# Another order of the last step and the tail, earlier accumulating masks and later casts in a top-k attention kernel with a squared-ReLU layer pair

## The chip, the cores and the metric

The kernel runs on one core of one Trainium2 chip. The metric is the device time of one execution in microseconds (us); lower is better. A core has a matrix engine (PE, with PEld for its weight loads), VectorE (DVE), ScalarE (ACT), GpSimd (POOL) and SyncE (SP), which work in parallel. Each takes its own instructions in order and waits for the others through semaphores. Transfers (DMA) are issued by SP, ACT or POOL and run beside the engines.

## The reference, cut to what matters

```python
# q, k, v: (8, 8, 576, 64), float32: batch, heads, rows, head size
scores = scale * np.matmul(q, k.transpose(0, 1, 3, 2))
kth = np.partition(scores, -32, axis=-1)[..., -32:-31]
scores = np.where(scores >= kth, scores, -1000000000.0)     # 32 largest of each row stay
attn = np.exp(scores - np.max(scores, axis=-1, keepdims=True))
attn = attn / (np.sum(attn, axis=-1, keepdims=True) + 1e-09)
x = heads_side_by_side(np.matmul(attn, v))                  # (4608, 512)
h = np.maximum(x @ w_in, 0.0)                               # w_in (512, 2048)
return h * h @ w_out                                        # w_out (2048, 512)
```

## The kernel before, in words

**Steps.** Two heads of a batch make a pair, 32 pairs in all; a pair has nine units of 64 or 128 rows. A step u takes two units at once (x = 0 and 1), and there are U = 144 steps, numbered 0 to 143. Every instruction is written down in a fixed order by the loop over u, and the order within an engine is the order of this program text. The work of one step's units is spread over five turns of the loop:

- in turn u − 1, `scores(u)`: PE multiplies q by k into two PSUM tiles (sc_a, sc_b), ACT copies them into s (L294); DVE's `pairs_of(u)` (L314, L315, and L317 while u is under `EARLY`, which is 11) and POOL's `both(u)` and `lesser(u)` (L338, L347) sort the scores into larger and smaller ones; from step 11 ACT's `copy_far(u)` (L330) moves a quarter of them.
- in turn u, `quads_of(u)` (L323, L324, the first instructions of a step on DVE) and `topk(u)`: four rounds of MAX8 (L373) and three of MATCH_REPLACE8 (L377) on DVE find the 32nd largest.
- in turn u + 1, `drop(u, x)`: ACT negates the maximum and the threshold (neg, L392), POOL writes bytes that mark the scores under the threshold (gone, L407), and these are added to s, which sends those scores far below zero. The addition is one of two: POOL adds by itself for each x (L409), as it does while u is under `EARLY`, or POOL issues one accumulating transfer for both x (L411).
- in turn u + 2, `exps(u, x)` on ACT (L415) and `turn(u)`, a transposing transfer issued by SP (L424).
- in turn u + 4, `products(u)`: PE multiplies by v (L459), `invert(u)` on DVE (reciprocal, L473) and `place(u)` on ACT (L489, L494), which writes the rows of x.

The last two steps are finished without transfers: ACT takes early exponentials (L400), DVE masks them (L419), PE transposes (`turn_by_tensor`, L441), and ACT or DVE copies the result (`turned`, L446, L448).

**q, k and v of a pair** are loaded by SP ahead of time. `prep_units` then gives four units, of which a turn of the loop takes one (two while u is under 8): q transposed, k transposed (`main`, L175), the rest rows (L213 to L216), and `values`, ACT's cast of v (L225). The casts of v's last 64 rows, `last_values` (L221), are put into the list `after_far` by `main` and are done at the end of the same turn.

**The layer pair.** When a chunk of 128 rows of x is complete, `x_unit` lets PE transpose it (L527, copied by ACT at L533 or DVE at L531), and `block` puts four first-layer pieces into `ups` (16 matmuls each, L574, then ReLU on ACT at L579 and the square, L585 on ACT or L583 on DVE). With the last of them four second-layer quarter pieces are put into `downs` (four matmuls each, L617, into the one PSUM tile dn_ps); after the fourth the result is copied (L625 on ACT, in the tail L623 on DVE) and stored by SP. `piece()` takes one entry, from `ups` and `downs` in turn; if the one is empty it takes from the other. With `piece(True)` the part after the matmuls is not done at once but is put into the list `behind`. During the steps `dense` calls `piece` in the gaps of the attention work.

**The tail** is the text after the loop: the products, reciprocals and placements of the last four steps (140 to 143), the last chunk's transposes, all pieces left, a reduction of flags on DVE (L855, which tells whether a slower general path must run), and the last chunk's second layer in two halves of 32 matmuls (L598), copied by DVE (L604) and ACT (L602).

Of the kernel before, what the change touches and what calls it, by code (L numbers as in the profile page):

```python
# [23 lines left out]
def kernel(  # L24
# [66 lines left out]
    raw, prep = {}, {}  # L91

    fetches = []
    after_far = []

    def by_head(t):
        return t.rearrange("p (a d) -> p a d", a=2)
# [61 lines left out]
    def prep_units(i):  # L159
        q_raw, k_raw, v_raw = raw[i]  # L160
        qkT = heads.tile([128, 512 + 640], f32, name="qkT")
        qT, kT = qkT[:, 0:512], qkT[:, 512:1152]
        k_rest = kT.rearrange("p (n d) -> p n d", d=64)[:, 0:10:9]
        bd, va = qbd[i % 5], vau[i % 6]
        prep[i] = (qT, kT, bd, va)

        def twice(t):
            return t.rearrange("p (o d) -> p o d", o=1).broadcast_to([128, 2, 64])

        def main(which, src):  # L170
            def go():
                tp = ps_one.tile([128, 512], f32, name="gen", bufs=2)
                for c in range(4):
                    pin(nc.tensor.transpose(tp[:, c * 128:(c + 1) * 128], src[:, c], id_f[:, :]))
                pin(nc.scalar.activation((qT, kT[:, 64:576])[which], tp[:, :], AF.Copy, scale=(scale, 1.0)[which]))  # L175
                after_far.append(lambda: last_values(which))
            return go


        def first_step():  # L180
            for j, bank in ((0, "gen"), (1, "gen"), (2, "dn_ps"), (3, "sc_a")):
                if bank == "sc_a":
                    tp = ps_sc.tile([128, 2, 512], f32, name=bank)[:, 0, :]
                else:
                    tp = ps_one.tile([128, 512], f32, name=bank, bufs=2 if bank == "gen" else None)
                if j < 2:
                    for c in range(2):
                        pin(nc.tensor.transpose(tp[:, c * 128:(c + 1) * 128], k_raw[:, 2 * j + c], id_f[:, :]))
                    to, got = kT[:, 64 + j * 256:64 + (j + 1) * 256], tp[:, 0:256]
                elif j == 2:  # L190
                    pin(nc.tensor.transpose(tp[:, 0:128], q_raw[:, 0], id_f[:, :]))
                    to, got = qT[:, 0:128], tp[:, 0:128]
                else:
                    pin(nc.tensor.transpose(tp[:, 0:64], k_raw[0:64, 4], id_f[0:64, 0:64]))
                    to, got = k_rest, twice(tp[:, 0:64])
                if j % 2:
                    pin(nc.vector.tensor_copy(to, got))
                else:
                    pin(nc.scalar.activation(to, got, AF.Copy, scale=scale if j == 2 else 1.0))

        def first_q():
            tp = ps_one.tile([128, 512], f32, name="gen", bufs=2)
            for c in range(1, 4):
                pin(nc.tensor.transpose(tp[:, c * 128:(c + 1) * 128], q_raw[:, c], id_f[:, :]))
            pin(nc.scalar.activation(qT[:, 128:512], tp[:, 128:512], AF.Copy, scale=scale))

        def rest(both=(0, 1)):
            tp = ps_one.tile([128, 512], f32, name="gen", bufs=2)
            for which in both:
                src = (q_raw, k_raw)[which]  # L210
                pin(nc.tensor.transpose(tp[:, which * 64:(which + 1) * 64], src[0:64, 4], id_f[0:64, 0:64]))
            if 0 in both:
                pin(nc.scalar.activation(bd[0:64, 0:64], tp[0:64, 0:64], AF.Copy, scale=scale))  # L213
                pin(nc.scalar.activation(bd[64:128, 64:128], tp[64:128, 0:64], AF.Copy, scale=scale))
            if 1 in both:
                pin(nc.scalar.activation(k_rest, twice(tp[:, 64:128]), AF.Copy))  # L216

        def last_values(x):
            assert i < 6 or av_left[i - 6] == 0
            half = slice(64 * x, 64 * x + 64)  # L220
            pin(nc.scalar.activation(va[half, 4 + x, :, 0:64], by_head(v_raw[half, 512:640]), AF.Copy))  # L221

        def values():
            assert i < 6 or av_left[i - 6] == 0
            pin(nc.scalar.activation(va[:, 0:4, :, 0:64], v_raw[:, 0:512].rearrange("p (a c d) -> p c a d", a=2, c=4), AF.Copy))  # L225

        def all_values():
            values()
            last_values(0)
            last_values(1)  # L230

        if i == 0:
            return [first_step, first_q, all_values, lambda: rest((0,))]
        return [main(0, q_raw), main(1, k_raw), rest, values]
# [115 lines left out]
    EARLY = 11  # L350
# [35 lines left out]
    def by_vector(u, x):  # L386
        return u == U - 1 or (u == U - 2 and x == 1)
# [14 lines left out]
    def drop(u, x):  # L402
        d = st[u]
        if x == 0:
            d["neg"] = negate(u, 2)
        s, byte = d["s"], gone[u % 2]
        pin(nc.gpsimd.tensor_scalar(byte[:, x, :, 1], s[:, x, :], scalar1=d["neg"][:, x, 1:2], scalar2=-HUGE, op0=ALU.add, op1=ALU.mult))  # L407
        if by_vector(u, 1) or u < EARLY:
            pin(nc.gpsimd.tensor_tensor(s[:, x, :], s[:, x, :], byte[:, x, :, :].rearrange("p n two -> p (n two)").bitcast(bf16), op=ALU.add))  # L409
        elif x == 1:  # L410
            pin(nc.gpsimd.dma_start(out=s[:, :, :].rearrange("p x n -> p (x n)"), in_=byte[:, :, :, :].rearrange("p x n two -> p (x n two)").bitcast(bf16), accum_op=ALU.add))  # L411
# [59 lines left out]
    def invert(u):  # L471
        r = small.tile([128, 2, 1], f32, name="rsum", bufs=4)
        pin(nc.vector.reciprocal(r[:, :, :], sums(u)[:, :, 64:65]))  # L473
        st[u]["r"] = r
# [265 lines left out]
    def ok(w):  # L740
        return 0 <= w < U
# [6 lines left out]
    def products(w):  # L748
        if ok(w):
            for x in range(2):  # L750
                weigh(w, x)
# [6 lines left out]
    for u in range(U):  # L758
        at_step[0] = u
        for x in range(2):  # L760
            if ok(u - 1) and not by_vector(u - 1, x):
                drop(u - 1, x)
        quads_of(u)
        topk(u, (0,))
        if u == U - 1:
            products(u - 4)
        if ok(u + 1):
            for i, c, a in steps[u + 1]:
                while coming <= i or (coming == i + 1 and soon):
                    prepare(u)  # L770
            scores(u + 1, (lambda: in_gap(u)) if u else None)
            both(u + 1)
        if u == 0:
            in_gap(u)
        if ok(u - 4):
            invert(u - 4)
        casts_next = bool(soon) and soon[0].__name__ == "values"
        for _ in range(0 if casts_next else 2 if u < 8 else 1):
            prepare(u)
        if ok(u - 4):  # L780
            place(u - 4)
        turn_x(u)
        moves.extend(soon_moves)
        soon_moves.clear()
        if u == U - 1:
            moves.pop(0)()()
        if ok(u - 2):
            exps(u - 2, 0)
            exps(u - 2, 1)
            turn(u - 2)  # L790
        fetch(4 if u < 12 else 3)
        topk(u, (1, 2))
        if ok(u + 1):
            pairs_of(u + 1)
            copy_far(u + 1)
            lesser(u + 1)
        topk(u, (3,))
        if casts_next:
            prepare(u)
        while after_far:  # L800
            after_far.pop(0)()
        if u == U - 2:
            early_exps(u, 1)
        if u < U - 1:
            dense(u, 0)
            dense(u, 1)
        else:
            early_exps(u, 0)
            exps(u - 1, 0)
            early_exps(u, 1)  # L810
            piece(True)
            piece(True)
        load_weights(1)
# [3 lines left out]
    while_scores.close()  # L817
    ends["pool"] = fast.enter_context(tc.tile_pool(name="ps_end", bufs=1, space=PSUM))

    def flush():  # L820
        if behind:
            behind.pop(0)()

    assert not fresh and not moves and not soon_moves
    late.append(True)
    products(U - 4)
    piece(True)
    behind.sort(key=lambda go: go.down)
    invert(U - 4)
    for u in (U - 2, U - 1):  # L830
        for x in range(2):
            turn_by_tensor(u, x)
            turned(u, x, u == U - 2)
    products(U - 2)
    products(U - 1)
    place(U - 4)
    products(U - 3)
    invert(U - 2)
    flush()
    place(U - 2)  # L840
    invert(U - 1)
    invert(U - 3)
    flush()
    place(U - 1)
    place(U - 3)
    rest = ups.pop(0)()
    turn_x(U)
    moves.pop(0)()()
    rest()
    while behind:  # L850
        flush()
    tail.append(0)
    while ups:
        ups.pop(0)()()
# [141 lines left out]
```

## Time and profile before

| what | value |
|---|---|
| median of three runs | 917.33 us |
| lowest and highest run | 914.49 and 920.94 us |
| the profiled execution's own time | 915.97 us |
| its span, from the first to the last instruction | 914.1 us |
| DVE busy | 882.7 us, 97% |
| ACT busy | 760.2 us, 83% |
| POOL busy | 777.6 us, 85% |
| PE busy | 675.0 us, 74% |

Rows of the timeline give the start in us, the duration in us, the engine (SPq and the like are an engine's queue of transfers), the line, the operation, output and input by the program's names with shapes, and a count where several instructions were merged; in brackets stands the idle time of the engine just before and what ended it. Rows of the table of stages give the stretch, its length, then busy time and number of instructions of PE, PEld, DVE, ACT and POOL, PE's granted clock (1.00 is full), the share of time that the DMA engines were busy, and GB/s.

### The profile page before, as it was taken

How to read it: one execution, taken by the hardware profiler on the slowest of the kernel's cores; microseconds unless marked ns; L12 is line 12 of the kernel's file. 1: busy time of each engine (PE TensorE's matmuls, PEld its weight loads, DVE VectorE, ACT ScalarE, POOL GpSimd, SP SyncE). 2: the span in 40 equal slices, each digit the busy share in tenths (PEclk: the TensorE clock that was granted, in tenths of full speed). 3: DMA queues.
4: the chain of work that ended last, by engine and by line, in shares of the span. 5: the costliest groups of instructions: out<-in, count | busy, mean ns of one | idle time of the engine just before them, and what ended most of it. 6: DMA issues, size and time to landing. Idle time of an engine off the chain costs nothing.

```text
span 914.1 us, 20885 instructions
## 1 busy us (share of the span) xinstructions
PE 675.0 (74%) x6188; PEld 427.2 (47%) x6264; DVE 882.7 (97%) x3632; ACT 760.2 (83%) x1755; POOL 777.6 (85%) x804
## 2 busy tenths in 40 slices
PE   6667667776786777777786777777777778878776
PEld 3333344544454445444454444454444445545454
DVE  5999999999999999999999999999999999999993
ACT  4566699889888998888987899988998888998881
POOL 7998989888988889888888888998898888888860
PEclk9999999899989999999989999999999999999999
DMA  7698799899998999899899998989989999788851
GB/s 145 106 165 142 155 184 202 192 198 194 193 202 185 196 198 195 190 175 215 178 198 182 202 199 186 205 193 196 185 192 197 199 202 196 156 166 172 163 117 39
DMA packets 290489, 163.60 MB, mean 179 GB/s; under 512 B 258112, under 2 KB 268608, under 8 KB 290368
## 3 DMA queue, kind: packets, MB, share of 16 engines
q1 hardware_dynamic: 267408, 80.29, 47.1%
q0 software_dynamic: 21616, 81.47, 40.0%
q8 instruction: 52, 0.85, 0.4%
q14 instruction: 69, 0.57, 0.2%
q10 hardware_dynamic: 1344, 0.43, 0.2%
HBM read 37.75 MB, written 9.44 MB: 52 GB/s over the span
## 4 chain that ended last, share of the span: by engine, by line
DVE 66%; issue 11%; PE 4%; DMA 3%; ACT 2%; POOL 2%; POOLq 0%; ACTq 0%
DVE m L373 27%; DVE cat L377 18%; DVE sc_b L314 6%; DVE cat L324 5%; DVE cat L323 5%; DVE most L315 4%; DMA s<-gone_a 1%; DMA s<-gone_b 1%; PE dn_ps L617 1%; DVE rsum L473 1%; PE gen L574 1%; PE sc_b L285 1%; POOL gone_b L407 0%; POOL cat L347 0%; PE end L598 0%
## 5 line engine op out<-in xcount | busy, mean ns | idle before, releaser
L373 DVE MAX8 m<-cat 128x8 f32<-128x104 f32 (+3 forms) x1152 | 438.7, 422 | 0.2 <-POOL cat L347 0.2
L377 DVE MATCH_REPLACE8 cat<-m,cat 128x104 f32<-128x104 f32 (+2 forms) x864 | 263.1, 312 | 0.0
L338 POOL TENSOR_TENSOR cat<-s 128x576 int32<-128x576 int32 (+1 forms) x144 | 238.6, 1657 | 3.1 <-ACT s L294 3.1
L347 POOL TENSOR_TENSOR cat<-cat,most 128x576 int32<-128x576 int32 (+1 forms) x144 | 195.8, 1360 | 19.6 <-ACT most L330 7.0
L285 PE MATMUL sc_b<-qkT 64*128 64x288 f32 x512 | 109.1, 501 | 95.3 <-DVE cat L324 91.2
L285 PE MATMUL sc_a<-qkT 64*128 64x288 f32 x512 | 98.2, 456 | 96.6 <-DVE most L315 62.9
L574 PEld LDWEIGHTS <-w_in 128*128 128x128 bf16 x2304 | 146.2, 101 | 39.0 <-issue 17.1
L617 PE MATMUL dn_ps<-w_out,h 128*128 128x512 bf16 x494 | 147.2, 420 | 10.3 <-issue 5.7
L294 ACT ACTIVATE s<-sc_b 128x576 f32<-128x576 f32 x144 | 93.4, 649 | 63.9 <-PE sc_b L285 57.0
L574 PE MATMUL gen<-xT,w_in 128*128 128x128 bf16 x2000 | 138.5, 226 | 2.6 <-ACT xT L533 1.4
L407 POOL TENSOR_SCALAR gone_a<-s,neg 128x576 uint8<-128x576 f32 x143 | 106.6, 745 | 21.3 <-ACT neg L392 10.8
L407 POOL TENSOR_SCALAR gone_b<-s,neg 128x576 uint8<-128x576 f32 x142 | 105.9, 746 | 18.3 <-ACT neg L392 7.7
L285 PEld LDWEIGHTS sc_a<-qkT 64*128 64x128 f32 x512 | 41.8, 188 | 124.2 <-issue 30.7
L285 PEld LDWEIGHTS sc_b<-qkT 64*128 64x128 f32 x512 | 44.7, 201 | 110.7 <-PE av_ps L459 64.1
L294 ACT ACTIVATE s<-sc_a 128x576 f32<-128x576 f32 x144 | 91.0, 632 | 3.3 <-DVE cat L317 1.7
L585 ACT ACTIVATE h<-rl 128x512 bf16<-128x512 f32 x136 | 85.7, 630 | 4.3
L579 ACT ACTIVATE rl<-gen 128x512 f32<-128x512 f32 x141 | 84.0, 596 | 2.4 <-PE gen L574 1.9
L617 PEld LDWEIGHTS <-h 128*128 128x128 bf16 x560 | 54.3, 106 | 66.2 <-issue 32.5
L459 PEld LDWEIGHTS <-wT 128*128 128x128 bf16 (+1 forms) x1600 | 54.9, 100 | 53.6 <-issue 43.9
L411 POOL DMA_DIRECT2D s<-gone_b x66 | 58.4, 884 | 21.7 <-DVE m L373 7.6
L415 ACT ACTIVATE w_two_a<-s,neg 128x576 bf16<-128x576 f32 x96 | 69.4, 781 | 6.7 <-DMA s<-gone_b 4.5
L415 ACT ACTIVATE w_two_c<-s,neg 128x576 bf16<-128x576 f32 x94 | 68.0, 781 | 8.1 <-DMA s<-gone_b 4.7
(170 smaller groups left out, 1203.1 us busy)
## 6 DMA issues: line engine op xcount, KB each, us to landing
s<-gone_b POOLq DMA_DIRECT2D x66, 576.0 KB, 4.6
s<-gone_a POOLq DMA_DIRECT2D x65, 576.0 KB, 4.7
v_raw<-in_v_dram SPq DMA_DIRECT2D x64, 128.0 KB, 3.1
k_raw<-in_k_dram SPq DMA_DIRECT2D x63, 128.0 KB, 3.3
q_raw<-in_q_dram SPq DMA_DIRECT2D x63, 128.0 KB, 3.2
out_dram<-wide SPq DMA_DIRECT2D x31, 256.0 KB, 3.1
v_raw<-in_v_dram SPq DMA_DIRECT2D x64, 32.0 KB, 3.1
w_in<-in_moe_w_in_dram POOLq DMA_DIRECT2D x8, 256.0 KB, 4.8
```

Source lines behind the costliest of these rows:

```text
L285: pin(nc.tensor.matmul(out=ps[j][:, x, 0:HALF], lhsT=lhsT, rhs=rhs, start=True, stop=True))
L294: pin(nc.scalar.activation(s[:, :, j * HALF:(j + 1) * HALF], ps[j][:, :, 0:HALF], AF.Copy))
L338: pin(tt(less, s[:, :, 0:wide].bitcast(i32), s[:, :, HALF:HALF + wide].bitcast(i32), op=ALU.add))
L347: pin(tt(less, less, d["most"][:, 0:n_h, :, :].bitcast(i32).rearrange("p h x n -> p x h n"), op=ALU.subtract))
L373: pin(nc.vector.max(out=m[r][:, x, :], in_=part(r, x)))
L377: pin(nc.vector.match_replace(out=part(r, x), in_to_replace=m[r][:, x, :], in_values=part(r, x), imm_value=NEG))
L407: pin(nc.gpsimd.tensor_scalar(byte[:, x, :, 1], s[:, x, :], scalar1=d["neg"][:, x, 1:2], scalar2=-HUGE, op0=ALU.add, op1=ALU.mult))
L415: pin(nc.scalar.activation(w_two[u % 3][:, x, 0:S], d["s"][:, x, :], AF.Exp, bias=d["neg"][:, x, 0:1]))
L574: pin(nc.tensor.matmul(out=hp[:, n * n_rows:(n + 1) * n_rows], lhsT=w_in[:, kh, (f0 + n) * 128:(f0 + n + 1) * 128], rhs=xt(kh), start=(kh ...
L579: pin(nc.scalar.activation(rl[:, :], hp, AF.Relu))
L585: pin(nc.scalar.activation(h2, flat, AF.Square))
L617: pin(nc.tensor.matmul(out=op[:, :], lhsT=held["h2"][:, f, c * 128:(c + 1) * 128], rhs=w_out[:, f, :], start=(f == 0), stop=(f == NF - 1)))
```

## The change

It has four parts. (1) `main` puts the casts of v's last rows into a second list, `next_far`, which becomes `after_far` at the end of the turn, so that they are done at the end of the next turn. (2) `drop` uses the accumulating transfer from unit step 9 on, whose mask is made in turn 10, instead of from unit step 11. (3) In the last turn two pieces are taken right after the products of step 139 and ahead of the last turned chunk but one; as the new assertion says, two first-layer pieces are then left in `behind` and two in `ups` at the end of the loop. (4) The tail has another order: the transposes of the last two steps stand ahead of the reciprocal of step 140, one piece fewer is taken there, and the deferred parts of the first-layer pieces stand between other instructions.

```diff
-    after_far = []
+    after_far, next_far = [], []
...
-                after_far.append(lambda: last_values(which))
+                next_far.append(lambda: last_values(which))
...
-        if by_vector(u, 1) or u < EARLY:
+        if by_vector(u, 1) or u < EARLY - 2:
...
         if u == U - 1:
             products(u - 4)
+            piece()
+            piece()
...
         while after_far:
             after_far.pop(0)()
+        after_far.extend(next_far)
+        next_far.clear()
...
-    def flush():
-        if behind:
-            behind.pop(0)()
-
-    assert not fresh and not moves and not soon_moves
+    assert not fresh and not moves and not soon_moves and len(behind) == 2 and len(ups) == 2
     late.append(True)
     products(U - 4)
-    piece(True)
-    behind.sort(key=lambda go: go.down)
-    invert(U - 4)
     for u in (U - 2, U - 1):
         for x in range(2):
             turn_by_tensor(u, x)
             turned(u, x, u == U - 2)
+    invert(U - 4)
     products(U - 2)
+    invert(U - 2)
     products(U - 1)
+    invert(U - 1)
+    behind.pop(0)()
     place(U - 4)
     products(U - 3)
-    invert(U - 2)
-    flush()
     place(U - 2)
-    invert(U - 1)
     invert(U - 3)
-    flush()
     place(U - 1)
     place(U - 3)
-    rest = ups.pop(0)()
+    behind.append(ups.pop(0)())
     turn_x(U)
     moves.pop(0)()()
-    rest()
+    behind.pop(0)()
+    behind.append(ups.pop(0)())
     while behind:
-        flush()
+        behind.pop(0)()
     tail.append(0)
     while ups:
         ups.pop(0)()()
```

## The prediction

> **What bounds the kernel now.** I read the page first, then the table of stages, then in the timeline the two places where VectorE is not busy.
>
> ```profile
> span 914.1 us, 20885 instructions
> PE 675.0 (74%) x6188; PEld 427.2 (47%) x6264; DVE 882.7 (97%) x3632; ACT 760.2 (83%) x1755; POOL 777.6 (85%) x804
> ```
>
> ```profile
> 76.00:114.00 38.00, 26.62 (x195) 14.63 (x196) 35.01 (x144) 26.45 (x66) 33.87 (x32) 0.96 0.71 137
> 114.00:300.00 186.00, 137.45 (x1306) 89.56 (x1322) 185.66 (x776) 165.84 (x386) 164.10 (x162) 0.94 0.93 195
> ```
>
> The third busy time of a stage row is DVE's. From 114 us on DVE is the clock: 185.66 of 186 us. There a change on ACT, POOL or PE brings nothing, and costs nothing while it stays in the shadow of DVE. From 76 to 114 DVE is busy for 35.01 of 38 us, so 3.0 us are open there. The rest of DVE's idle time lies before the first scores, which no edit touches, and in the tail.
>
> The hole between 76 and 114 us, in the timeline:
>
> ```profile
> 74.47 0.44 DVE L323 TENSOR_TENSOR cat<-sc_b,most 128x288 f32<-128x288 f32 x1
> 79.02 0.47 DVE L314 TENSOR_TENSOR sc_b<-sc_a,s 128x288 f32<-128x288 f32 x1 [0.52 <-ACT s L294]
> 81.52 0.46 DVE L323 TENSOR_TENSOR cat<-sc_b,most 128x288 f32<-128x288 f32 x1 [0.35 <-ACT most L330]
> 92.46 1.42 DVE L373 MAX8 m<-cat 128x8 f32<-128x576 f32 x2 [0.16 <-POOL cat L347]
> 100.42 0.46 DVE L323 TENSOR_TENSOR cat<-sc_b,most 128x288 f32<-128x288 f32 x1 [0.54 <-ACT most L330]
> 107.93 0.46 DVE L323 TENSOR_TENSOR cat<-sc_b,most 128x288 f32<-128x288 f32 x1 [1.41 <-ACT most L330]
> 113.95 0.44 DVE L323 TENSOR_TENSOR cat<-sc_b,most 128x288 f32<-128x288 f32 x1
> 119.95 0.43 DVE L323 TENSOR_TENSOR cat<-sc_b,most 128x288 f32<-128x288 f32 x1
> ```
>
> L323 is the first DVE instruction of a step. 74.47 is step 10, 113.95 step 16, 119.95 step 17. An undisturbed step takes 6.00 us (113.95 to 119.95); the six from 74.47 to 113.95 took 39.48, so 3.48 us too long, of which 0.52 + 0.35 + 0.16 + 0.54 + 1.41 = 2.98 us are waits that the trace names. Their cause stands on ACT and POOL:
>
> ```profile
> 77.51 0.32 ACT L221 ACTIVATE vau_e<-v_raw 64x128 bf16<-64x128 f32 x1 [4.83 <-DMA v_raw<-in_v_dram]
> ```
>
> ```profile
> 78.02 0.75 POOL L407 TENSOR_SCALAR gone_b<-s,neg 128x576 uint8<-128x576 f32 x1 [1.19 <-ACT neg L392]
> 85.27 0.75 POOL L407 TENSOR_SCALAR gone_a<-s,neg 128x576 uint8<-128x576 f32 x1
> 89.53 1.40 POOL L338 TENSOR_TENSOR cat<-s 128x576 int32<-128x576 int32 x1
> 92.52 1.57 POOL L407 TENSOR_SCALAR gone_b<-s,neg 128x576 uint8<-128x576 f32 x2
> 98.39 1.56 POOL L407 TENSOR_SCALAR gone_a<-s,neg 128x576 uint8<-128x576 f32 x2
> 100.89 1.72 POOL L338 TENSOR_TENSOR cat<-s 128x576 int32<-128x576 int32 x1
> 115.73 1.56 POOL L407 TENSOR_SCALAR gone_b<-s,neg 128x576 uint8<-128x576 f32 x2
> ```
>
> ACT, in order, sat 4.83 us on the cast of v's last rows because their transfer had not landed. Behind it stood neg of step 9, and POOL idled for it. POOL then did steps 9 and 10 with its own two adds: from 85.27 to 89.53, 4.26 us until the next step's L338, where a step with the accumulating transfer takes 98.39 to 100.89, 2.50 us. The mask of step 11 began at 92.52, about 5 us after its step; at 115.73 it is 1.8 us after 113.95. A late mask makes late exponentials on ACT, a late L330 behind them, and DVE waits for L330.
>
> **The tail.** PE is followed here.
>
> ```profile
> 876.06 1.89 PE L617 MATMUL dn_ps<-w_out,h 128*128 128x512 bf16 x7
> 881.24 0.52 ACT L489 ACTIVATE x_tok<-av_ps,rsum 128x64 bf16<-128x64 f32 x2 [0.68 <-DVE rsum L473]
> 881.61 0.43 PE L527 MATMUL gen<-id_h,x_tok 128*128 128x128 bf16 x2 [3.24 <-ACT x_tok L489]
> 882.73 1.86 PE L574 MATMUL gen<-xT,w_in 128*128 128x128 bf16 x16 [0.69 <-ACT xT L533]
> 884.39 1.82 PE L617 MATMUL dn_ps<-w_out,h 128*128 128x512 bf16 x4
> 885.50 1.76 DVE L419 SCALAR_TENSOR_TENSOR w_two_c<-s,m,e 128x576 bf16<-128x576 f32 x2
> 891.37 0.55 PE L527 MATMUL end<-id_h,x_tok 128*128 128x128 bf16 x4 [0.51 <-ACT x_tok L489]
> 895.32 1.06 PE L574 MATMUL end<-xT,w_in 128*128 128x128 bf16 x16
> 896.43 0.81 PE L617 MATMUL dn_ps<-w_out,h 128*128 128x512 bf16 x3
> 897.66 1.34 DVE L855 TENSOR_REDUCE worst<-flags 128x1 f32<-128x1152 f32 x1
> 899.11 0.69 DVE L623 COPY wide<-dn_ps 128x512 f32<-128x512 f32 x1
> 899.86 5.17 PE L617 MATMUL dn_ps<-w_out,h 128*128 128x512 bf16 x16 [2.62 <-DVE wide L623]
> 905.09 3.67 PE L598 MATMUL end<-w_out,h 128*128 128x256 bf16 x32
> ```
>
> ```profile
> 899.80:903.20 3.40, 3.34 (x9) 1.19 (x9) 0.01 (x1) 0.00 (x0) 0.00 (x0) 0.52 0.35 77
> ```
>
> Two quarter pieces of an older chunk's second layer are left for the last step. One runs at 884.39, the other only at 896.43, after all first-layer pieces. Its result sits in the one dn_ps buffer; DVE first does the reduction L855 and only then the copy L623, and the next 16 matmuls wait 2.62 us for that buffer. After the pause PE's granted clock is 0.52, and nine matmuls take 3.34 us. From 905.09 + 3.67 = 908.76 to the end of the span are 5.3 us of copy, transfer and closing that no edit touches.
>
> **The change part by part.** *v's casts a step later.* The instructions are the same, 0.31 us each. The cast that waited until 77.51 moves behind the work of step 10, near 80 us, where its data lie. The 4.83 us wait goes; nothing queued behind it is late.
>
> *Accumulating from step 10.* It removes four POOL adds and adds two transfers: 4.26 − 2.50 = 1.76 us a step, 3.5 us of POOL over two steps. That with the 1.19 us of idling covers the 3.2 us (5.0 − 1.8) by which the mask of step 11 was later than in the steady state. So the backlog is not there and L330 is on time. What is new is that ACT's exponentials of steps 9 and 10 wait for a landing:
>
> ```profile
> s<-gone_b POOLq DMA_DIRECT2D x66, 576.0 KB, 4.6
> ```
>
> With neg on time the first transfer is issued near 79 and lands near 83.5. ACT asks for such data 2.7 us into a step,
>
> ```profile
> 116.67 1.45 ACT L415 ACTIVATE w_two_c<-s,neg 128x576 bf16<-128x576 f32 x2
> ```
>
> as here behind 113.95; in step 11 that is also about 83.3, with slack behind it (below). I price it at nothing; if it lands late, by what follows under the rivals. For the hole I take 3.2 us, between the named 2.98 and the whole 3.48; as bounds 1.0 (half of ACT's L330 waits stay) and 3.5.
>
> [...] POOL's transfer instructions do wait for DVE here, at the longest
>
> ```profile
> 660.15 0.88 POOL L411 DMA_DIRECT2D s<-gone_b  x1 [1.51 <-DVE most L315]
> ```
>
> [...]
>
> *The two leftovers in front.* Eight matmuls move to 878.25, right after the products of step 139, into the 3.24 us that PE idles until 881.61. Warm, eight such take 1.89 us (876.06, seven of them recorded), so PE is through at 880.2. The result is copied by ACT, where DVE took 0.69 us for such a copy (899.11), in the 0.68 us that ACT idled before 881.24; its output transfer passes SP's queue before the next transpose. Price nothing. If the clock is low there, a quarter takes 1.82 us as at 884.39, PE is through at 881.9, the copy ends near 882.6 and everything behind moves by 1.3 us, but DVE's masks at 885.50 end at 887.26 whatever PE does, so at most 1.0 us comes through.
>
> *The middle of the tail.* With only first-layer pieces in step 143, PE is free before the masks end; transposes, ACT's copies and the four placements come earlier, and the reciprocal of step 140 later. Masks end at 887.26. The last five transposes (four of L527 took 0.55), DVE's copy of them and a reciprocal I estimate at 1.4 us together, from those lengths. Four placements by ACT at 0.52 (881.24) end at 890.8, and L527 starts 0.5 us before its 891.37. One more first-layer piece stands behind it as before (five in both), so 0.3 us arrive at the last of them (bounds −0.3 and 0.7).
>
> *The end.* After the last first-layer piece PE goes straight into the 16 matmuls: no quarter piece, no wait, and dn_ps has been free since step 143. At the warm pace, 0.213 us each from 876.06 (1.89 for eight with some 0.19 of drain), they take 3.42, with the counting matmul 3.55. So L598 starts at 896.43 + 3.55 = 899.98 instead of 905.09: 5.1 us, of which 3.4 are the quarter piece and the wait and 1.7 the clock. L855 ends by 899 as now, before the count needs it. With 0.3 from above 5.4 us; bounds 3.4 (clock stays low) and 5.9.
>
> *Moved casts over the rest of the run:* nothing, bounds −0.5 and +1.5 (next part).
>
> **Sum.** 3.2 + 5.4 = 8.6 us. The profiled execution took 915.97 us, giving 907.4; it lies 1.4 below the median of the three runs, from which the sum gives 908.7. I say 907.8, between the two.
>
> **The rivals.** *(A) The backlog stays.* The two new transfers wait behind DVE for up to 1.51 us each, or land late, and ACT's L330 is late in steps 12 to 14 just as in 13 to 15 now. For it: DVE's largest wait, 1.41 us, arose in steps that already had the transfer. Against: POOL was then 3 us behind. Of 3.2 us some 0.5 are left, the tail pays: 917.3 − 5.9 = 911.4.
>
> *(B) The wait at the end is replaced.* PE's clock stays low through the 16 matmuls (5.17 us), or the copy of ACT at 881 holds the placements. The tail brings 3.4 and less 1.0: 917.3 − 3.2 − 2.4 = 911.7. For it: the clock at 899.8 fell after only 2.62 us of idling. Against: PE has no such gap after 891.
>
> *(C) Slower: the casts collide with the rest rows.*
>
> ```profile
> 118.44 0.41 ACT L330 ACTIVATE most<-sc_b 128x288 f32<-128x288 f32 x1 [0.32 <-DVE sc_b L314]
> ```
>
> ```profile
> L221 ACT ACTIVATE vau_a<-v_raw x12: 301/309/321, 12.3 to 757.8; 64x128 bf16<-64x128 f32 x12
> ```
>
> A cast now falls in the step that already has the small copies of the remaining rows. If ACT were full there, neg, mask and the next L330 would be late by 0.31 us and DVE with them. L330 ends at 118.85 and DVE wants it at 119.95: 1.1 us of slack, so this decides only where ACT is over 1 us behind. Were all 62 casts paid in full, 19 us less 8.6: 928. Even half of them (9.6) ends at 918.3, slower. ACT's 165.84 of 186 us speaks against it.
>
> **How the numbers follow.** Forecast 0.75, A 0.10, B 0.08, C 0.07. A measurement of this kernel tells about 1%, 9.2 us, from no change, and the forecast lies 0.4 us beyond that line, which is 908.16. With the spread of the runs (914.49 to 920.94) some 0.64 of the forecast case falls beyond the line: 0.48 of faster. The rest of it, A and B make 0.46 of within 1%; C, less its mildest outcomes, 0.06 of slower. The range takes in A and B: 904.0 to 913.0. Its low end is the best bounds together (3.5 + 5.9 + 0.5 = 9.9 us, 906.1) and 2 us of the runs' spread.
>
> **What would show it.** Right: no ACT wait for v_raw near 77 us; L323 of step 16 near 110.5; a mask of step 11 within 2 us of its step; two quarters of L617 near 878 and ACT's copy before 881.24; the last 16 L617 in under 3.8 us with no wait before them; L598 near 899.7; the span near 905.5. Wrong: L330 waits between 80 and 110 us (A), a granted clock near 0.5 after 896 (B), new DVE waits for ACT once a pair between 114 and 878 (C).

## The result, and the profile after

Six runs of each kernel: 919.71 us (914.49 to 920.94) before and 908.64 us (908.06 to 910.22) after. The ratio is 0.9892, interval [0.9867, 0.9917]: 11.1 us faster. The profiled execution of the changed kernel took 908.94 us, against the 915.97 us of the one shown before. The page of after, its span and first part:

```profile
span 906.6 us, 20887 instructions
PE 669.6 (74%) x6188; PEld 426.3 (47%) x6264; DVE 881.8 (97%) x3631; ACT 762.4 (84%) x1756; POOL 773.9 (85%) x802
```

VectorE has the same work, 882 us; what is gone is idle time. The table of stages of after, for the hole and for the middle of the run (DVE is the third busy time):

```profile
76.00:110.80 34.80, 26.80 (x195) 14.59 (x196) 34.66 (x143) 25.43 (x63) 31.40 (x31) 0.95 1.00 204
110.80:876.00 765.20, 569.17 (x5452) 368.44 (x5520) 762.67 (x3176) 681.10 (x1566) 669.76 (x656) 0.95 0.91 190
```

The hole is shut: DVE is busy for 34.66 of 34.80 us. The timeline of after at that place:

```profile
74.60 0.21 ACT L392 ACTIVATE neg<-m 128x4 f32<-128x4 f32 x1 [1.91 <-DVE m L373]
79.23 0.31 ACT L221 ACTIVATE vau_e<-v_raw 64x128 bf16<-64x128 f32 x1
84.79 1.44 ACT L415 ACTIVATE w_two_a<-s,neg 128x576 bf16<-128x576 f32 x2 [0.96 <-DMA s<-gone_b]
88.62 1.56 POOL L407 TENSOR_SCALAR gone_b<-s,neg 128x576 uint8<-128x576 f32 x2
110.81 0.45 DVE L323 TENSOR_TENSOR cat<-sc_b,most 128x288 f32<-128x288 f32 x1
876.27 0.48 DVE L323 TENSOR_TENSOR cat<-sc_b,most 128x288 f32<-128x288 f32 x1
```

The cast at 79.23 waits for nothing. The mask of step 11 begins at 88.62; before it was at 92.52. Step 16 begins at 110.81 where it began at 113.95: 3.14 us gained. Step 143 begins at 876.27 where it began at 879.52: 3.25 us. Between those two points nothing was won or lost (765.46 against 765.57 us). The exponentials of steps 9 and 10 now wait for a landing (0.96 us here, 0.29 us in the next step), and DVE does not feel it in this execution.

The tail of after:

```profile
877.32 1.04 PE L617 MATMUL dn_ps<-w_out,h 128*128 128x512 bf16 x4 [1.41 <-ACT h L585]
878.39 0.60 ACT L625 ACTIVATE wide<-dn_ps 128x512 f32<-128x512 f32 x1 [1.03 <-PE dn_ps L617]
878.88 0.51 ACT L489 ACTIVATE x_tok<-av_ps,rsum 128x64 bf16<-128x64 f32 x2
880.43 3.57 PE L574 MATMUL gen<-xT,w_in 128*128 128x128 bf16 x32 [0.69 <-ACT xT L533]
883.97 0.82 DVE L419 SCALAR_TENSOR_TENSOR w_two_c<-s,m,e 128x576 bf16<-128x576 f32 x1 [0.43 <-ACT e L400]
893.05 1.06 PE L574 MATMUL gen<-xT,w_in 128*128 128x128 bf16 x16
894.16 3.40 PE L617 MATMUL dn_ps<-w_out,h 128*128 128x512 bf16 x15
897.61 3.67 PE L598 MATMUL end<-w_out,h 128*128 128x256 bf16 x32
```

From the last first-layer piece to L598 are 4.56 us (893.05 to 897.61), where they were 9.77 (895.32 to 905.09): 5.21 us gained, with no wait left and 16 matmuls (15 recorded) at a granted clock of 1.00, where it was 0.52 through nine of them before. But the last first-layer piece itself is late. Measured from L323 of the last step it begins at 16.77 us; before at 15.81. So 4.26 us of the 5.21 reach the end. The sum for these two executions is 3.14 + 0.11 + 4.26 = 7.5 us, the difference of the spans (914.1 and 906.6). The medians differ by 11.1. The experiments had to find what took 1 us of the tail, and where the medians' other 3.6 us are.

### The profile page after: what moved, and what is told of

Its sections match the earlier page's. It is cut to its first block, busy times and chain, and to the rows that moved or that the text cites. A ratio compares the mean times of both kernels' runs of the same rounds, so it can differ in the third digit from the quotient of the medians.

```text
span 906.6 us, 20887 instructions
## 1 busy us (share of the span) xinstructions
PE 669.6 (74%) x6188; PEld 426.3 (47%) x6264; DVE 881.8 (97%) x3631; ACT 762.4 (84%) x1756; POOL 773.9 (85%) x802
## 4 chain that ended last, share of the span: by engine, by line
DVE 71%; issue 11%; PE 6%; ACT 4%; DMA 4%; POOL 2%; SPq 1%; POOLq 0%; ACTq 0%; DVEq 0%
DVE m L373 29%; DVE cat L377 19%; DVE sc_b L314 6%; DVE cat L324 5%; DVE cat L323 5%; DVE most L315 5%; DMA s<-gone_a 1%; PE sc_b L285 1%; DMA s<-gone_b 1%; PE gen L574 1%; DVE rsum L473 1%; PE dn_ps L617 1%; PE sc_a L285 1%; DMA v_raw<-in_v_dram 1%; ACT x_tok L489 1%
## 5 line engine op out<-in xcount | busy, mean ns | idle before, releaser
L373 DVE MAX8 m<-cat 128x8 f32<-128x104 f32 (+3 forms) x1152 | 449.8, 441 | 0.0
L377 DVE MATCH_REPLACE8 cat<-m,cat 128x104 f32<-128x104 f32 (+2 forms) x864 | 271.1, 331 | 0.0
L285 PE MATMUL sc_b<-qkT 64*128 64x288 f32 x512 | 106.0, 488 | 93.1 <-DVE cat L324 89.1
L574 PEld LDWEIGHTS <-w_in 128*128 128x128 bf16 x2304 | 148.0, 102 | 39.1 <-issue 17.0
L617 PE MATMUL dn_ps<-w_out,h 128*128 128x512 bf16 x494 | 142.7, 409 | 8.8 <-issue 5.2
L574 PE MATMUL gen<-xT,w_in 128*128 128x128 bf16 x2016 | 140.6, 227 | 2.7 <-ACT xT L533 1.6
L377 DVE MATCH_VALUE_LOAD cat<-m,cat 128x8 f32 x864 | 82.6, 96 | 0.0
L411 POOL DMA_DIRECT2D s<-gone_a x66 | 58.3, 883 | 20.5 <-DVE cat L377 9.0
```

Source lines behind the costliest of these rows:

```text
L285: pin(nc.tensor.matmul(out=ps[j][:, x, 0:HALF], lhsT=lhsT, rhs=rhs, start=True, stop=True))
L373: pin(nc.vector.max(out=m[r][:, x, :], in_=part(r, x)))
L377: pin(nc.vector.match_replace(out=part(r, x), in_to_replace=m[r][:, x, :], in_values=part(r, x), imm_value=NEG))
L574: pin(nc.tensor.matmul(out=hp[:, n * n_rows:(n + 1) * n_rows], lhsT=w_in[:, kh, (f0 + n) * 128:(f0 + n + 1) * 128], rhs=xt(kh), start=(kh ...
L617: pin(nc.tensor.matmul(out=op[:, :], lhsT=held["h2"][:, f, c * 128:(c + 1) * 128], rhs=w_out[:, f, :], start=(f == 0), stop=(f == NF - 1)))
```

## The experiments

The same few points, read from each trace's timeline (us). "Steps 10 to 16" is the stretch of the hole (six steps, 36.0 undisturbed); the last four columns count from L323 of step 143.

| kernel | steps 10 to 16 | 16 to 143 | masks end | last L574 begins | L598 begins | end |
|---|---|---|---|---|---|---|
| before | 39.48 | 765.57 | 7.75 | 15.81 | 25.57 | 34.61 |
| b_again | 38.93 | 770.46 | 7.75 | 16.95 | 26.84 | 35.81 |
| e1_casts | 37.67 | 771.40 | 7.77 | 15.91 | 25.80 | 34.90 |
| e2_masks | 37.85 | 768.46 | 7.76 | 16.70 | 26.58 | 35.72 |
| e3_casts_masks | 37.60 | 763.80 | 7.76 | 16.92 | 26.81 | 35.87 |
| after | 36.35 | 765.47 | 8.52 | 16.77 | 21.34 | 30.35 |
| a_again | 36.47 | 764.64 | 8.45 | 15.57 | 20.13 | 29.24 |
| e4_tail | 39.71 | 770.86 | 8.45 | 15.71 | 20.27 | 29.39 |
| e6_copy_later | 35.97 | 767.32 | 7.80 | 14.92 | 19.48 | 28.53 |
| e7_old_order | 36.00 | 763.21 | 8.48 | 15.27 | 19.83 | 28.75 |
| b_apart | 39.86 | 772.22 | 7.76 | 15.70 | 25.40 | 34.41 |
| e5_before_busy | 39.55 | 766.74 | 7.75 | 16.96 | 25.16 | 34.24 |
| best_apart | 36.55 | 763.72 | 7.76 | 14.77 | 19.33 | 28.33 |

**The kernel before, once more** (b_again, no edit).

> The kernel before once more, with a second profile. Its runs lay between 914.49 and 920.94 us, its profile at 915.97, the changed kernel's between 908.06 and 910.22. Theory: the spread comes from the hole between 76 and 114 us, whose length hangs on when v's rows land and how far GpSimd then lags; a profile of a slower execution shows a longer hole (over 5 us of VectorE waits instead of 2.98), and the middle and the tail as in the first. Rival: the spread lies outside the hole (other stalls between 114 and 878 us); then the hole is 3.0 again. Time 915 to 921 either way.

Measured: 920.13 us, ratio 1.0017 [0.9993, 1.0041]; its executions lie between 914.93 and 923.2. The profiled one took 5 us longer than the one shown, but its hole was no longer than before (38.93 us): the stall lies elsewhere, as the rival had it. The timeline names one place:

```profile
660.78 0.88 POOL L411 DMA_DIRECT2D s<-gone_b  x1 [1.51 <-DVE most L315]
660.82 1.29 SPq L424 DMA_TRANSPOSE wT<-w_two_c  x1
671.40 1.44 ACT L415 ACTIVATE w_two_a<-s,neg 128x576 bf16<-128x576 f32 x2 [5.97 <-DMA s<-gone_b]
673.17 0.46 DVE L323 TENSOR_TENSOR cat<-sc_b,most 128x288 f32<-128x288 f32 x1 [5.09 <-ACT most L330]
```

The transfers of b_again that were issued from 660 to 676 us, with their median time to landing in the last column:

```profile
s<-gone_b POOLq DMA_DIRECT2D x1, 576.0 KB, 10.6
...
k_raw<-in_k_dram SPq DMA_DIRECT2D x2, 128.0 KB, 8.9
...
wT<-w_two_c SPq DMA_TRANSPOSE x1, 10.8
```

The accumulating transfer was issued 0.04 us before the transposing one, and both landed after 10.6 and 10.8 us instead of some 4.7. ACT waited 5.97 us and DVE 5.09. In the profile shown of before the same transfer begins at 660.15 and the transpose only 1.07 us later:

```profile
661.22 2.21 SPq L424 DMA_TRANSPOSE wT<-w_two_c  x1
```

There the accumulating transfer landed after 4.7 us and nobody waited. This stood in no step of the prediction.

**v's casts alone** (e1_casts, in the kernel before).

```diff
-    after_far = []
+    after_far, next_far = [], []
...
-                after_far.append(lambda: last_values(which))
+                next_far.append(lambda: last_values(which))
...
+        after_far.extend(next_far)
+        next_far.clear()
```

> The kernel before with v's last casts moved by a step, and nothing else. Theory (two causes, each with its part): ACT's 4.83 us wait goes, neg of step 9 is on time, VectorE's 0.52 and 0.35 us go, but GpSimd still makes two masks by its own adds with the wide sorting, starts the mask of step 11 about 5 us behind its step, and the waits of 0.16, 0.54 and 1.41 us stay: 0.9 us faster than before, some 2.3 us of the hole left. Rival (the late cast alone is the cause): the whole hole of 3.1 us closes. Second rival (GpSimd's adds alone): nothing gained.

**The accumulating mask from step 10 alone** (e2_masks, in the kernel before).

```diff
-        if by_vector(u, 1) or u < EARLY:
+        if by_vector(u, 1) or u < EARLY - 2:
```

> The kernel before with the accumulating transfer from step 10 on, and nothing else. Theory: the wait of ACT for v's rows stays 4.8 us and with it VectorE's waits of 0.52 and 0.35 us; GpSimd saves 3.5 us over two steps and starts the mask of step 11 within 2 us of its step, so the 0.16, 0.54 and 1.41 us go: 2.1 us faster. Rival (the late cast alone): nothing gained, the waits of 0.54 and 1.41 stay.

**Both, with the old tail** (e3_casts_masks).

> Both of these, with the old last step and tail. Theory: the hole closes as in the changed kernel, step 16 begins near 110.8 us instead of 113.95; 3.1 us faster than the profiled execution before, the tail from the last turn's start as before. If the spread of the kernel before comes from the hole, its runs lie within 2 us of each other, and against the median of before it gains 5 to 7 us. Rival: the two parts work on the same wait, and together bring no more than the larger alone.

Measured, in the hole: of 39.48 us (38.93 in b_again) the casts leave 37.67, the masks 37.85, so each closes about half (0.9 and 2.1 us had been expected of them). With the casts moved, all of DVE's named waits but the largest are gone; with the masks alone ACT still sits 5.1 us on the late cast, and DVE waits 0.81, 0.35 and 0.38. One row of e1_casts, then two of e2_masks, both from the timeline:

```profile
107.04 0.46 DVE L323 TENSOR_TENSOR cat<-sc_b,most 128x288 f32<-128x288 f32 x1 [1.50 <-ACT most L330]
```

```profile
79.19 0.47 DVE L314 TENSOR_TENSOR sc_b<-sc_a,s 128x288 f32<-128x288 f32 x1 [0.81 <-ACT s L294]
94.18 0.46 DVE L323 TENSOR_TENSOR cat<-sc_b,most 128x288 f32<-128x288 f32 x1 [0.38 <-ACT most L330]
```

e3_casts_masks had 37.60 in its profiled execution, of which 1.52 us are one wait for L330; without it 36.1. Behind that wait stands the first of the two new accumulating transfers, issued at 78.09, which landed only after 7.46 us:

```profile
85.58 1.44 ACT L415 ACTIVATE w_two_a<-s,neg 128x576 bf16<-128x576 f32 x2 [2.49 <-DMA s<-gone_b]
87.34 0.46 DVE L323 TENSOR_TENSOR cat<-sc_b,most 128x288 f32<-128x288 f32 x1 [1.52 <-ACT most L330]
```

Total times: e1 919.97 us, ratio 1.0000 [0.9974, 1.0026]; e2 915.24, 0.9959 [0.9932, 0.9987]; e3 913.06, 0.9935 [0.9908, 0.9961]. These do not follow the hole: e1 closes half of it and is no faster, and e3 wins 6 us by a hole of 2 to 3. The column "16 to 143" suggests why: in their profiled executions e1 and e2 had a stall as in b_again (accumulating transfers of 12.0 and 11.4 us), e3 had none. e1's twelve executions lie in two groups, three at 913.26 to 914.09 and nine at 918.56 to 921.12.

**The changed kernel once more, and its tail alone** (a_again: no edit; e4_tail: the changed kernel with both edits of the hole undone).

> The changed kernel once more, beside the next three, with a second profile. Its tail, from the last turn's first VectorE instruction to the end, should again be 30.3 us (906.6 less 876.3). In the profiles so far one long VectorE wait of 5 to 6.5 us near 660 us stands wherever GpSimd's accumulating transfer and SyncE's transposing one were issued within 0.06 us of each other (three profiles of three), and nowhere else. Theory: that meeting, not the hole, makes the spread of the kernel before, and the changed kernel's runs stay within 3 us because its phases do not meet. Rival: the changed kernel meets as well, now and then, and some of its runs lie 5 us above the others.

> The kernel before with the new last turn and tail alone (casts and masks as before). Theory: the hole between 76 and 114 us is there with 3 us of waits; the tail gains 4.2 us as in the changed kernel: 5.2 at the end (quarter piece, wait and clock), less 1.0 in its middle. Runs that meet no stall of transfers near 911, others some 5 us above. Rival: the tail's gain is 5.4 us as predicted, and the loss in the middle belongs to something that the casts or masks moved.

Measured: a_again 910.03 us, 0.9901 [0.9869, 0.9933], its six executions in two groups, 906.64 to 908.23 and 911.83 to 913.03; so the rival came here, and the changed kernel, too, probably meets a stall now and then. e4_tail 915.05 us, 0.9945 [0.9924, 0.9966], with a stall in the profiled execution and a tail of 29.39 us, 5.2 us shorter than that of before; here, too, it is the rival that came (5.4), not the theory (4.2). By their medians, stalls included, either half of the change alone is worth a good half per cent: 0.9935 and 0.9945.

a_again's tail ends 1.1 us sooner than after's with the same instructions. The table of stages shows PE's granted clock (third from the right), first of after and then of a_again:

```profile
880.00:882.00 2.00, 1.57 (x16) 1.57 (x16) 2.00 (x4) 1.97 (x5) 0.33 (x2) 0.50 0.60 131
882.00:884.00 2.00, 2.00 (x23) 2.00 (x22) 1.31 (x3) 1.94 (x3) 1.56 (x3) 0.50 0.57 114
884.00:886.00 2.00, 2.00 (x26) 2.00 (x24) 0.82 (x2) 0.99 (x2) 0.00 (x0) 0.50 0.23 46
```

```profile
880.00:882.00 2.00, 1.62 (x30) 1.62 (x30) 2.00 (x4) 1.97 (x5) 0.34 (x2) 1.00 0.59 131
882.00:884.00 2.00, 1.35 (x29) 1.23 (x26) 1.29 (x3) 2.00 (x4) 1.78 (x3) 1.00 0.61 119
884.00:886.00 2.00, 1.22 (x29) 0.93 (x26) 1.71 (x5) 1.56 (x4) 0.00 (x0) 1.00 0.20 41
```

Step 143 begins at the same time in both (876.27 and 876.28), PE's pauses up to 880.4 us are the same, and yet the clock falls in one of them, to 0.50 from 879.44 to 886.27: 16 first-layer matmuls from 880 to 882 us in the one, 30 in the other. The price is 1.2 us (L598 at 21.34 or 20.13). The kernel before pays it too: b_again's clock was at 0.50 for 6.8 us as well, and its L598 comes 1.27 us after that of the profile shown, where the low stretch was 3.4 us long.

**The copy later, and the old order** (both in the changed kernel).

```diff
             piece()
-            piece()
+            piece(True)
+            copy_left = behind.pop()
...
+            copy_left()
```

> The changed kernel, but ACT's copy of the older chunk's second-layer result stands behind the last early exponential instead of ahead of the placement of step 139. Theory: in the changed kernel that copy waits on ACT for the last quarter piece, which waits 1.4 us for the square of the chunk's last first-layer piece, and so holds placement, transpose, exponentials and masks by 0.9 us. Here the placement starts 1.7 us after the turn's first VectorE instruction as in the kernel before, the masks no longer wait for ACT, and L598 starts 0.9 us earlier: 0.9 us faster than the changed kernel. Rival: PE's low clock through the two first-layer pieces sets the end of the middle; then ACT's copy is out of the way and at most 0.2 us are gained.

```diff
+    invert(U - 4)
     for u in (U - 2, U - 1):
...
-    behind.append(ups.pop(0)())
+    rest = ups.pop(0)()
     turn_x(U)
     moves.pop(0)()()
-    behind.pop(0)()
-    behind.append(ups.pop(0)())
-    while behind:
-        behind.pop(0)()
+    rest()
+    ups.pop(0)()()
```

(e7_old_order; the reciprocals and the deferred parts, too, stand where the tail before had them.)

> The changed kernel with the leftovers in front as there, but with the tail's instructions in the old order (reciprocal of step 140 ahead of the last copies, deferred parts between placements). Theory: the gain lies in the leftovers' place alone, the new order is worth within 0.4 us either way. Rival: the new order brings the 0.5 us that the prediction gave it, and this kernel is that much slower than the changed one.

Measured against a_again (whose granted clock is 1.00 from 876 to 890 us; the first 32 first-layer matmuls take 1.95 us in it and in e7; for e6 a full clock is assumed): with the copy later the masks end at 7.80 instead of 8.45 and L598 begins 0.65 us sooner (0.9 had been expected); with the old order 0.30 us sooner. So ACT's copy at 878.39 did hold the placement and the exponentials behind it, and the new order of the tail costs some 0.3 us rather than gaining it. Set on top of the later copy, in best_apart below (which also has the small transfers), the old order gains 0.15 (19.48 to 19.33), so this price is known to no better than a factor of two. Total times: e6 911.05 us, 0.9902 [0.9872, 0.9932], its twelve executions spread from 905.24 to 920.91, with a stall at 452 us in the profiled one; e7 906.43 us, 0.9885 [0.9846, 0.9924], its executions at 904.79 to 907.13 and at 911.99 and 914.78. Neither total tells 0.3 or 0.65 us apart; the tails in the traces do.

**The transpose pushed back** (b_apart: in the kernel before, a transfer of two bytes ahead of each transpose in SP's queue).

```diff
+        pin(nc.sync.dma_start(out=spare[0:1, 0:1], in_=w_two[u % 3][0:1, 1, S - 1:S]))
```

> The kernel before, with one more transfer of a single element on SyncE ahead of every transposing transfer, waiting for the same exponentials, so that each transposing transfer is issued some 0.6 us later. In ten profiles with 1322 accumulating transfers the five whose transposing transfer was issued between 0.02 us before and 0.06 us after them took 9.9 to 12.0 us, and every VectorE wait over 4 us stands there; next in line are transfers with a transposing one 0.1 us before or 0.18 us behind, which took 4.7 to 7.5 us. Only one of 1322 lies 0.5 to 0.7 us before, so that a delay of 0.6 us should leave almost no meeting. Theory (the meeting causes the stall): no accumulating transfer over 9 us in the profile, and most runs of this kernel lie at 914 to 917 us where most of before lie at 918 to 923. Rival (the stall comes with the place near 660 us, not with the meeting): runs at 918 to 923 stay the majority.

Measured: 922.18 us, 1.0007 [0.9982, 1.0033]; five executions at 916.37 to 917.89, the others at 922.09 or more. The expectation missed: seven of twelve executions took 922 us or more, and the profile has a transfer over 9 us. The place near 661 us was free, but the push of 0.65 us moved another pair onto each other:

```profile
673.98 0.89 POOL L412 DMA_DIRECT2D s<-gone_b  x1 [0.30 <-POOL gone_b L408]
674.00 1.29 SPq L426 DMA_TRANSPOSE wT<-w_two_b  x1
```

```profile
s<-gone_b POOLq DMA_DIRECT2D x1, 576.0 KB, 10.9
```

The transfer took 10.9 us and DVE waited 5.83. In the profile shown of before this was the one pair whose transpose came 0.65 us ahead of the accumulating transfer, at 672.70. Pushing all transposes shifted the meeting here; it didn't abolish it.

**Transfers alone** (probe: 200 rounds of one mask, one accumulating and one transposing transfer, with an ACT instruction whose length grows from round to round and so sweeps the offset between the two; a load of one head's rows is added in every second round, all other work is left out, and the output is zeros).

> None of the computation, only the two transfers by themselves: 200 rounds, in each GpSimd does two mask instructions and then issues the accumulating transfer, while ScalarE writes the exponentials' tile, the second time in a growing width (64 to 1054 columns, about 0.01 us more every two rounds), and SyncE then issues the transposing transfer. Every second round a load of one head's rows is issued first. The output is zeros. Theory: in the rounds in which the two are issued within 0.06 us of each other, both take 9 us or more, and all others under 8 us. Rival: the meeting is harmless by itself, and every round's transfers take 3 to 8 us; then more of the kernel's traffic is needed.

Rounds in order, in the probe's timeline; DVE's wait is for the accumulating transfer. First a round with the transpose 0.8 us ahead, then the last round but one:

```profile
22.99 1.28 SPq L65 DMA_TRANSPOSE wT<-w_two  x1
23.77 0.89 POOL L64 DMA_DIRECT2D s<-gone  x1 [0.30 <-POOL gone L63]
29.09 0.17 DVE L56 COPY pad<-s 128x8 f32<-128x8 f32 x1 [7.19 <-DMA s<-gone]
...
1542.67 0.89 POOL L64 DMA_DIRECT2D s<-gone  x1 [0.30 <-POOL gone L63]
1542.71 1.27 SPq L65 DMA_TRANSPOSE wT<-w_two  x1
1552.51 0.17 DVE L56 COPY pad<-s 128x8 f32<-128x8 f32 x1 [11.71 <-DMA s<-gone]
```

and the transfers issued from 23 to 29 us, then those from 1541 to 1553 us:

```profile
s<-gone POOLq DMA_DIRECT2D x1, 576.0 KB, 5.2
wT<-w_two SPq DMA_TRANSPOSE x1, 3.2
```

```profile
s<-gone POOLq DMA_DIRECT2D x1, 576.0 KB, 9.7
wT<-w_two SPq DMA_TRANSPOSE x1, 9.9
```

By offset (transpose minus accumulating issue), the accumulating transfer first and the transposing one behind it: −0.77 us: 4.8 to 5.7 and 3.2 us; −0.3: 5.1 to 5.6 and 4.2 to 4.7; −0.06 to −0.02: 5.7 to 6.0 and 5.6 to 6.2; 0.00: 7.0 to 7.6 and 7.2 to 7.9; +0.02: 8.1 to 8.2 and 8.3 to 8.4; +0.03: 8.1 to 9.2 and 8.3 to 9.3; +0.04, a single round: 9.7 and 9.9. So the two transfers slowed each other without the rest of the kernel, but the expectation came in part only: both transfers reached 9 us in the last two rounds alone, and with the transpose 0.06 to 0.02 us ahead they took 6.2 us at most. The sweep ended there, still rising, so the far side of the window is seen only in the kernels: in ten of their traces the stalled transfers lie at up to +0.06, and the next offset, +0.18, took 7.5 us at most.

**PE kept busy before the last 16** (e5_before_busy: in the kernel before, 12 matmuls into an unused tile while the 16 wait for their buffer).

> The kernel before with 12 matmuls more (512 columns, results unused) on PE between the last quarter piece and the 16 matmuls that wait for VectorE's copy. Theory: the 2.6 us wait stays, but PE's granted clock does not fall, and the 16 matmuls take 3.4 to 3.6 us instead of 5.2, so that L598 starts 1.7 us earlier after the last first-layer piece (8.1 us instead of 9.8). Rival: the slow matmuls do not come from the idle time; then 9.8 us stay.

The timeline of e5_before_busy:

```profile
897.92 1.06 PE L574 MATMUL end<-xT,w_in 128*128 128x128 bf16 x16
899.68 2.75 PE L862 MATMUL gen<-fill,id_h 128*128 128x512 bf16 x12
902.46 3.61 PE L617 MATMUL dn_ps<-w_out,h 128*128 128x512 bf16 x16
906.12 3.67 PE L598 MATMUL end<-w_out,h 128*128 128x256 bf16 x32
```

The same 16 matmuls take 3.61 us instead of 5.17, and L598 begins 8.20 us after the last first-layer piece instead of 9.77: those 1.6 us go with the clock of 0.52 in the kernel before (899.8 to 903.2 us), as the prediction had split it (1.7); 3.61 is the pace of a_again, too (3.62). In total 916.54 us, 0.9951 [0.9933, 0.9968]. That is 4.5 us, more than the 1.6 that the trace explains; its nine executions (913.79 to 918.74) may have met the stall less often, though nothing ahead of the tail was edited.

**All together** (best_apart: the changed kernel with the old order, the copy later, and b_apart's small transfer).

> The changed kernel with three more edits: ACT's copy behind the last early exponential, the tail's instructions in the old order, and the single-element transfer ahead of every transposing one. Theory: the first two bring 0.6 and 0.3 us in the tail, the third takes away the stall of 5 us, so that the runs lie close together at 904 to 907 us, under those of the changed kernel (906.6 to 913.0 in the last comparison). Rival: SyncE is late with its loads through the additional transfers, ACT waits for v's rows again, and 1 to 3 us are lost.

Measured: 905.76 us, five executions from 905.53 to 906.5, ratio 0.9841 [0.9827, 0.9855]: the fastest kernel here, and the one with the narrowest spread. Its longest accumulating transfer took 7.2 us. Five executions without a stall do not show that the small transfer prevents it; in b_apart it did not. The tail's timeline of best_apart has PE at the pace that a_again shows at a clock of 1.00 (32 first-layer matmuls in 1.95 us):

```profile
878.89 1.95 PE L576 MATMUL gen<-xT,w_in 128*128 128x128 bf16 x32 [0.69 <-ACT xT L535]
894.99 3.67 PE L600 MATMUL end<-w_out,h 128*128 128x256 bf16 x32
```

## Why the prediction was right, point by point

**The hole, 3.2 us.** Right: 3.14 us by the two profiles. The five profiles with the old hole (before, b_again, e4, b_apart, e5) average 39.5 us for the six steps, the five with both edits and the changed tail 36.3: 3.2 us; with e3_casts_masks 36.5, and 3.0. The mechanism was as told: no ACT wait for v, POOL's mask of step 11 back in pace, the L330 waits gone; and the two edits share it half and half. The landing at no price was mis-sized. It was put at the usual 4.6 us and took 5.93 in after, so that it came 0.96 us after ACT had asked. That cost DVE nothing there and 1.52 us in e3_casts_masks, where it took 7.46; in this the second half of rival A's condition ("or land late") did come, in one profile of six.

The pause of 1.51 us ahead of one of POOL's transfers, which rival A took as its bound, did not decide: the six transfers of the stretch in after waited 0.3 us each, while 1.51 us stand at 660.78 in b_again, as at 660.15 in the profile before. Nor is it shown that such a pause is a wait for VectorE, as the row names it: in the probe, where VectorE stands idle meanwhile, 60.5 us stand ahead of 199 of the 200 transfers, 0.30 us each on average, and 2.3 us ahead of the other. The lasting backlog of rival A did not come. The 0.5 us that it left of the hole's 3.2 was the author's estimate, and no run shows it: after gained 3.14 us there, and e3_casts_masks, with its late landing, still 1.88 (39.48 to 37.60).

**The leftovers at no price.** Too low. The second quarter piece had to wait 1.41 us for ACT's square of the last rows' chunk, so the copy began at 878.39 and held the placement, the early exponentials and the masks: 8.45 us instead of 7.75. The copy was to be done ahead of the placement at 881.24, which is 877.99 on the changed kernel's time (3.25 us earlier); it ended at 878.99. The prediction had the masks end at 887.26 "whatever PE does"; they ended 0.7 us later because ACT, which writes their exponentials, was late. e6_copy_later puts the price at 0.65 us. The prediction had seen the way (at most 1.0, by a low clock) but not the cause: it looked at when PE was free and not at when the piece's input was made.

**The middle of the tail, +0.3 us.** Right only in sum. The last first-layer piece begins 0.1 to 0.2 us sooner when like is compared with like: 16.95 in b_again and 16.77 in after, each with 6.8 us at a clock of 0.50; 15.81 before, with 3.4 us of it, and 15.71 in e4_tail, for which the same is assumed. Inside that, the copy costs 0.65 and the new order 0.15 to 0.3 us, so by difference, which no run shows by itself, the pieces taken out of the tail are worth about 1. In the profile shown of after it looks like a loss of 1 us, because PE's clock was at 0.50 for 6.8 us there and for 3.4 in the one shown of before; that is the variation of 1.2 us that both kernels show, and no term of the prediction.

**The end, 5.1 us.** Right: 5.21, of which 1.6 go with the low clock by e5_before_busy. The tail as a whole came to 5.3 to 5.5 by the same pairs (25.57 to 20.27, 26.84 to 21.34 for L598: 5.30 and 5.50), as forecast. (The sign "L598 near 899.7" had left out the 3.2 us of the hole; with them it is 896.5, and L598 began at 897.61.) Rival B, that the clock stays low through the 16 matmuls or the copy holds the placements, came in its second half only, at 0.65 us.

**The moved casts over the rest, nothing.** Right for DVE's waits: in after all waits for L330 from 110.80 to 876 us are 0.7 us together, none over 0.24. Rival C did not come. But the step that took the middle of the run as fixed was wrong. From step 16 to 143 the thirteen traces take 763.2 to 766.7 us without a stalled pair of transfers and 767.3 to 772.2 with one, and the times suggest that the kernel before often has one: 918.0 us or more were taken by 16 of its 32 executions beside b_again, by 16 of 19 beside a_again and by 17 of 20 beside b_apart. The 32 spread from 914.41 to 924.49 without a clear gap, so the share is a guess.

**The sum.** 8.6 us were forecast from one profiled execution that had met no stall, and 907.8 from two bases; the median came to 908.64. The gain between medians is 11.1 us. Hole and tail explain 8.6 of it by the averages above; that the rest is stalls met less often fits the groups of times and the profiles, but only profiled executions show a stall, so its share of the medians is inferred. Why the changed kernel meets less often was not settled: e6_copy_later has the same middle and met one at 452 us. So the forecast time was close partly by luck: the base of 917.3 was low for the kernel before (919.71 over six runs), and the gain was forecast too small.

## What to carry to other kernels

Price a moved piece by the moment its input is made, not by the gap it is to fill; and see who stands behind its copy on that engine. When the runs of one kernel spread by 1% and the profile shows no cause, profile it again: the cause may be in the execution that was not seen. Two transfers whose starts drift against each other met at 452, 661, 669 and 674 us in the traces here, and a constant delay only moved the place.

## What the runs showed of the hardware

**An accumulating transfer of GpSimd and a transposing transfer of SyncE that started within some 0.05 us of each other stalled here.** In ten traces with 1322 accumulating transfers, five were issued between 0.06 us before and 0.01 us after a transpose's issue: all five took 9.9 to 12.0 us (b_again 10.6, e1 12.0, e2 11.4, e4 11.8, e6 9.9); no other exceeded 9.05 us, and the few over 8.1 stood right behind a stalled one. b_apart adds a sixth, 10.9. The probe puts the near edge at about the same instant: with the transpose 0.02 us ahead 5.7 to 6.0 us, at 0.00 7.0 and more. Plain loads and stores were issued within 0.08 us of an accumulating transfer in 49 cases, none over 7.3 us. Other transfers of the core were slow meanwhile: in the rows of 660 to 676 us in b_again, two loads of k took 9.7 and 8.2 us, where the median of its 63 loads of k of that size is 3.5. What inside the transfer engines does it is open.

**PE's clock fell in one execution and not in the next, over the same pauses.** From 874 to 880.4 us PE's longest pause is 1.41 us in after and 1.40 in a_again, and the clock was 0.50 for 6.8 us in the one and 1.00 in the other; L598 then began 1.2 us later in the one. In the profile before it was 0.52 from 899.8 to 903.2 us, behind a pause of 2.62 us, and with that pause filled with matmuls in e5_before_busy the 16 behind it took 3.61 us instead of 5.17. What decides when the clock falls is not shown.
